# Hash attention and PReLU MLP: signs of a pair in one ScalarE pass placed by transfers, weights rounded with integer adds, GpSimd's adding transfer and small copies moved to VectorE

## The chip, the cores and the metric

The kernel runs on one core of a Trainium2 chip. The core has a matrix engine (TensorE, with its weight loads shown apart as PEld), VectorE (DVE), ScalarE (ACT), GpSimd (POOL) and SyncE (SP), which here only issues transfers. The metric is the device time of one execution in microseconds, the median of several runs. A profile of one execution gives, for every instruction, its engine, source line, start and duration, and for every transfer its time from issue to landing.

## The reference

Attention in which a query sees only the keys whose six hash bits equal its own, followed by a two-layer MLP with a per-channel PReLU:

```python
batch, n_heads, seq, head_dim = (4, 8, 768, 64)          # proj: (64, 6)
q_bits = (np.einsum('bhsd,dk->bhsk', q, proj) > 0)
k_bits = (np.einsum('bhsd,dk->bhsk', k, proj) > 0)
mask = q_bucket[:, :, :, None] == k_bucket[:, :, None, :]   # bucket: the six bits as a number
scores = np.where(mask, scale * q @ k.T, -1000000000.0)
attn = softmax(scores);  attn_out = attn @ v
x = attn_out.transpose(0, 2, 1, 3).reshape(B * S, H * D)    # 3072 x 512
h = x @ w_in                                                # 512 x 2048
g = np.maximum(h, 0.0) + alpha * np.minimum(h, 0.0)
out = (g @ w_out).astype(np.float32)                        # 2048 x 512
```

The two weight matrices come as 64-bit floats; everything else is fp32. The kernel therefore rounds the weights to fp32 itself, from the low and high 32-bit words of each number.

## The kernel before

All that runs is `fast_path`; a flag that it computes would start `general_path` for inputs out of range, which these inputs are not.

**Attention.** The work goes over 16 pairs of heads (4 batches x 4 pairs), numbered from 0 here. Two heads share the 128 partitions. For each pair, in the order in which each engine runs it:

- `turn` (L669) transposes `q` and `k` on TensorE into `qT` and `kT`, two pairs ahead.
- `hash_bits` (L689), one pair ahead, multiplies them with the projection into one two-bank PSUM tile `hs`, in blocks of 32 rows that hold `k` and `q` of the two heads, the blocks of the second half of the sequence swapped between heads. Then signs are taken: `qb` and `kb` are +-1 numbers in bf16. ScalarE does it for all pairs from 1 on in seven instructions, four for `qb` (L712) and three for `kb` (L723), since each block must land at its own partitions. Pair 0 (`engine is DVE`) uses ScalarE for `qb` and VectorE for `kb` (L719).
- `scores` (L726) makes 12 cells of 128 keys x 384 queries. In each cell a bf16 product of the signs and the fp32 product of `qT` and `kT` (L734) are added in PSUM, then ScalarE takes the exponential (L737). Cells go key block by key block, and for each both query halves: cell 0 needs the first half of `qb`, cell 1 the second half; cells 6 to 11 need the second half of `kb`. Score tiles, transposes, hash products and row sums share three two-bank PSUM tiles in rotation.
- The row sums of the exponentials are added up on VectorE: `add_first` (L743), `add_third` (L754), `add_last` (L749), `add_total` (L758). In `add_first` from pair 1 on, GpSimd also issues a transfer that adds half of the third block into `accp` (L747), so `add_third` covers only the other half.
- `attend` (L762) multiplies with `v` (L770); `totals` (L776) sums `accd` over keys on TensorE (`sm`, L784); `divide` (L789) turns the sums into factors with VectorE transposes, reciprocals, four 32x12 copies on GpSimd (L806, L807) and a multiplication (L817), and stores `x`.

**Weights.** Between these steps, two of 32 pieces of 128x512 weights are rounded per pair. A piece goes through `load_weight` (L561), `weight_abs` (L574, on ScalarE except for the first two), `weight_clamp` (L583), `weight_parts` (L589) and `weight_sum` (L600). `weight_parts` shifts the absolute value of the high word into fp32 form (L594), takes its exponent (L597) and scales the low word with it (L598); `weight_sum` adds the two in fp32 (L619) and puts the sign in (L624). `weight_group` (L630) stores finished groups of `w_out` (L636) and queues sums and stores of groups of `w_in`.

**MLP.** After the last pair the two products are computed with a seven-product scheme in blocks, from the stored `x`, `w_in` and `w_out`. The change doesn't touch this stage.

**Order.** Compute instructions keep the written order on each engine (`do` is `keep_in_program_order`). Transfers are placed by the scheduler; SyncE issues them strictly in its own order, and each waits on SyncE for its data and buffers, so that one waiting transfer holds all behind it. Tiles come from pools with a fixed number of buffers (two unless stated); a tile's buffer is taken over only when the users of its last tile are done.

Of the kernel before, what the change touches and what calls it, by code (L numbers as in the profile page):

```python
# [8 lines left out]
F32 = mybir.dt.float32  # L9
BF16 = mybir.dt.bfloat16  # L10
U32 = mybir.dt.uint32
AF = mybir.ActivationFunctionType
ALU = mybir.AluOpType

# [392 lines left out]
def fast_path(  # L407
# [12 lines left out]
    nc = tc.nc  # L420
# [80 lines left out]

    def setup():

        zero = pool.tile([P, 512], BF16, name="zero", bufs=1)
        do(DVE.memset(zero, 0.0))
        do(DVE.memset(wh, 0.0))
        for s in range(2):
            nc.sync.dma_start(wh[D * s : D * s + D, :NB], proj)
        nc.sync.dma_start(alpha16, moe_alpha.rearrange("(t p) -> t p", p=P))
        make_identity(nc, ident)  # L510
        do(DVE.memset(ones, 1.0))

        ps = psum_av.tile([P, 2, 512], F32, name="nil", tag="av")
        nil.append(lambda: do(PE.matmul(ps[:, 0], zero[:, :P], zero, start=True, stop=True)))
        for i in range(7):
            nil[0]()

        do(DVE.memset(hb, 0.0))
        for r in range(0, P, 32):
            do(DVE.memset(hb[r : r + 2 * NB], 1.0 if r % D else -1.0))  # L520
            do(DVE.memset(hb[r : r + NB], -1e-37))

        do(DVE.tensor_scalar(hb_k[:, 0:1], hb, -1.0, None, op0=ALU.mult))
        do(DVE.memset(hb_k[:, 1:2], 0.0))
        for r in range(0, P, 32):
            do(DVE.memset(hb_k[r : r + 2 * NB, 1:2], 0.5))
        for t in pts:
            do(POOL.memset(t[:, :, :, CW : CW + 1], 1.0))
        for t in qbs:
            do(POOL.memset(t, 0.0))  # L530
# [36 lines left out]
    def halves(i):  # L567
        words = raw[i].bitcast(U32).rearrange("p (f t) -> p f t", t=2)
        return words[:, :, 0], words[:, :, 1]
# [4 lines left out]
    def weight_abs(i, engine=None):  # L574
        i = order[i]
        lo, hi = halves(i)
        wx[i] = pool.tile([P, 512], F32, name=f"wx{i}", tag="wx")
        if engine is DVE:
            do(DVE.tensor_scalar(wx[i].bitcast(U32), hi, 0x7FFFFFFF, None, op0=ALU.bitwise_and))
            return  # L580
        do(ACT.activation(wx[i], hi.bitcast(F32), AF.Abs))

# [5 lines left out]

    def weight_parts(i):  # L589
        i = order[i]  # L590
        lo, hi = halves(i)
        x = wx[i]
        wr[i] = r = pool.tile([P, 512], F32, name=f"wr{i}", tag="wr", bufs=1)
        do(DVE.tensor_scalar(  # L594
            x.bitcast(U32), x.bitcast(U32), 3, 0xC0000000, op0=ALU.logical_shift_left, op1=ALU.bitwise_xor,
        ))
        do(DVE.tensor_scalar(r.bitcast(U32), x.bitcast(U32), 0x7F800000, None, op0=ALU.bitwise_and))  # L597
        do(DVE.scalar_tensor_tensor(r, lo, 2.0 ** -52, r, op0=ALU.mult, op1=ALU.mult))  # L598

    def weight_sum(i):  # L600


        i = order[i]
        lo, hi = halves(i)
        x, r = wx[i], wr[i]
        if i < HW:
            n, m = divmod(i, 4)
            if m == 0:
                wst[n] = pool.tile([P, NM, 4, P], F32, name=f"wsi{n}", tag="wsi")
            slot = (0, 5, 1, 2)[m]  # L610
            dst = wst[n][:, slot].rearrange("p i f -> p (i f)")
        else:
            n, m = divmod(i - HW, 2)
            if m == 0:
                wst[HW + n] = pool.tile([P, 4, DM // 2], F32, name=f"wso{n}", tag="wso")
            w = wst[HW + n]
            dst = w[:, 0:4:3] if m == 0 else w[:, 1:3]
        turned = i < HW and m == 3
        do(DVE.scalar_tensor_tensor(  # L619
            r, x, -1.0 if turned else 1.0, r, op0=ALU.mult, op1=ALU.subtract if turned else ALU.add,  # L620
        ))
        if i >= HW:
            hi, r = (t.rearrange("p (a f) -> p a f", a=2) for t in (hi, r))
        do(DVE.scalar_tensor_tensor(  # L624
            dst.bitcast(U32), hi, 0x80000000, r.bitcast(U32), op0=ALU.bitwise_and, op1=ALU.bitwise_xor,
        ))

    sums_due = []

# [59 lines left out]
    def hash_bits(pi, halves=BOTH, engine=None):  # L689

        if halves.start == 0:
            bits["q", pi] = qbs[pi % 2]
            bits["k", pi] = pool.tile([P, S], BF16, name=f"kb{pi}", tag="kb")
        ps = {"k": two_banks(f"hs{pi}")}
        ps["q"] = psum_av.tile([P, 2, 512], F32, name=f"hsq{pi}", tag="av") if engine is DVE else ps["k"]
        for half in range(halves.start, halves.stop):
            for name in "qk" if engine is DVE else "kq":
                for s in range(2):  # L700
                    r, c = D * s, D * (s ^ half) + 32 * "kq".index(name)

                    for t, c in [("k", c)] + ([("q", c ^ D)] if engine is DVE and name == "q" else []):
                        do(PE.matmul(  # L704
                            ps[t][c : c + 32, half if t == "k" or engine is not DVE else 0, :CW], wh[r : r + D],
                            tr[name, pi][r : r + D, half * CW : (half + 1) * CW], start=True, stop=True,
                        ))
        for half in range(halves.start, halves.stop):
            cols = slice(half * CW, (half + 1) * CW)
            for s in range(2):  # L710
                c = D * (s ^ half ^ (engine is DVE)) + 32
                do(ACT.activation(  # L712
                    bits["q", pi][D * s : D * s + 32, cols], ps["q"][c : c + 32, 0 if engine is DVE else half, :CW], AF.Sign, bias=hb[c : c + 32],
                ))

            for to, c, n in [(0, 0, P)] if half == 0 else [(0, D, D), (D, 0, D)]:
                dst, src = bits["k", pi][to : to + n, cols], ps["k"][c : c + n, half, :CW]
                if engine is DVE:
                    do(DVE.tensor_scalar(  # L719
                        dst, src, hb_k[c : c + n, 0:1], hb_k[c : c + n, 1:2], op0=ALU.is_gt, op1=ALU.subtract,  # L720
                    ))
                else:
                    do(ACT.activation(dst, src, AF.Sign, bias=hb[c : c + n]))  # L723


    def scores(pi, cells):  # L726
# [16 lines left out]
    def add_first(pi):  # L743
        accp[pi] = pool.tile([P, 2 * NCH, CW], F32, name=f"accp{pi}", tag="accp", bufs=1)
        do(DVE.tensor_tensor(accp[pi], p(0), p(1), op=ALU.add))  # L745
        if pi:
            nc.gpsimd.dma_start(accp[pi][:, 2:], p(2)[:, 2:], accum_op=ALU.add)  # L747

    def add_last(pi):  # L749
        accd[pi] = pool.tile([P, 2 * NCH, CW], F32, name=f"accd{pi}", tag="accd", bufs=1)  # L750
# [1 line left out]
        do(DVE.tensor_tensor(accd[pi], accd[pi], p(5), op=ALU.add))  # L752

    def add_third(pi):  # L754
        n = 2 if pi else 4
        do(DVE.tensor_tensor(accp[pi][:, :n], accp[pi][:, :n], p(2)[:, :n], op=ALU.add))

    def add_total(pi):  # L758
        do(DVE.tensor_tensor(accd[pi], accd[pi], accp[pi], op=ALU.add))  # L759
# [29 lines left out]
    def divide(pi, between=lambda: None):  # L789

        b, hp = pairs[pi]
        n = HW2 // 32
        a = pool.tile([P, NCH, HW2], F32, name=f"st{pi}", tag="st", bufs=1)
        r = pool.tile([P, NCH, n], F32, name=f"rc{pi}", tag="rc")
        rr = pool.tile([P, NCH, 2, n], F32, name=f"rr{pi}", tag="rr")
        d = pool.tile([P, NCH, CW], F32, name=f"dn{pi}", tag="dn", bufs=1)
        for g in range(NCH):
            do(DVE.transpose(a[:, g], sums[pi][:, g, :HW2]))  # L800
        do(DVE.tensor_scalar(r, a.rearrange("p g (n w) -> p g n w", w=32)[:, :, :, 0], S * EPS, None, op0=ALU.add))
        for h in range(2):
            do(DVE.reciprocal(rr[:, :, h], r))
        for q0 in (0, D):
            q1 = q0 + 32
            do(POOL.tensor_copy(rr[q0 : q0 + 32, :, 1], rr[q1 : q1 + 32, :, 1]))  # L806
            do(POOL.tensor_copy(rr[q1 : q1 + 32, :, 0], rr[q0 : q0 + 32, :, 0]))  # L807
        vsum[pi] = pool.tile([P, 1], F32, name=f"vs{pi}", tag="vs")
        do(DVE.tensor_scalar(vsum[pi], av[pi][:, 0, CW : CW + 1], EPS, None, op0=ALU.mult))
        between()  # L810
        do(DVE.transpose(
            d.rearrange("p g w -> p (g w)"),
            rr.rearrange("p g h n -> p (g h n)").unsqueeze(2).to_broadcast([P, 2 * NCH * n, 32]),
        ))

        x = mid.tile([P, NCH, CW], F32, name=f"x{pi}", tag="x", bufs=1)
        do(DVE.scalar_tensor_tensor(x, av[pi][:, :, :CW], vsum[pi], d, op0=ALU.add, op1=ALU.mult))  # L817
        nc.sync.dma_start(x_s[b, hp], x.rearrange("p g w -> p (g w)"))
# [471 lines left out]
```

## Time and profile before

| | |
|---|---|
| median of 3 runs | 893.71 us (893.67 to 894.51) |
| profiled execution, span from first to last instruction | 892.6 us |
| busy in the span: TensorE, VectorE, ScalarE, GpSimd | 882.5, 756.4, 407.2, 46.2 us |
| attention stage, one pair | 20.6 us, 16 pairs up to 338 us |
| transfers: SyncE's queue, GpSimd's queue | 123.64 MB, 14.29 MB |
| granted TensorE clock | 0.998 of full speed |

In a line of groups or of a timeline, `out<-in` are tile names without numbers, followed by the shape; `xN` is a count. In a line of a timeline the first two numbers are the start and the duration in us, and brackets give idle time before the instruction and who ended it. A line of waits gives who waited for whom, the total in us, how many times and the longest. `SPq` is SyncE issuing a transfer; its duration is the issue alone. Durations of matmuls are modelled, and a busy TensorE is not one at its peak.

### The profile page before, as it was taken

Reading aid. Unit: us, or ns where it says so; the run is one execution under the profiler, and the core shown is the slowest. Engines: PE = TensorE matmul, PEld = TensorE weight load, DVE = VectorE, ACT = ScalarE, POOL = GpSimd, SP = SyncE. Lnnn points to the kernel's source line nnn. Section 1 sums busy time; section 2 is a strip of 40 time slices with the busy share of each in tenths; the row PEclk is TensorE's granted clock in tenths of the full one; section 3 lists DMA queues with packets and bytes.
Section 4 is the critical chain, followed back from the end, with each engine's and each line's share of the span. In section 5 each row is a group of like instructions: output and inputs, shape, how many; then the busy total and the mean of one; then the engine's idle time right before and its main releaser. Section 6 shows DMA issues by size and latency. Waiting matters only on the chain.

```text
span 892.6 us, 15369 instructions
## 1 busy us (share of the span) xinstructions
PE 882.5 (99%) x5886; PEld 594.4 (67%) x5886; DVE 756.4 (85%) x1266; ACT 407.2 (46%) x726; POOL 46.2 (5%) x109
## 2 busy tenths in 40 slices
PE   9999999999999999999999999999999999999996
PEld 5444445555554445557997557997557997556996
DVE  6888988989999987899898678988668988768986
ACT  7888888888888862222112222112222112222111
POOL 1000000100110001110000000000000000000000
PEclk9999999999999999999999999999999999999999
DMA  8565586686796826587334334333425242530242
GB/s 231 138 164 137 160 231 167 173 237 191 205 291 175 229 69 217 179 292 282 136 104 135 137 125 153 133 122 103 168 96 182 96 158 81 166 108 0 95 149 68
DMA packets 124978, 140.17 MB, mean 157 GB/s; under 512 B 77776, under 2 KB 109024, under 8 KB 121312
## 3 DMA queue, kind: packets, MB, share of 16 engines
q1 hardware_dynamic: 116096, 123.64, 44.2%
q0 software_dynamic: 6384, 14.29, 6.5%
q10 hardware_dynamic: 2416, 1.18, 0.5%
q8 instruction: 48, 0.79, 0.4%
q14 instruction: 34, 0.28, 0.1%
HBM read 104.87 MB, written 28.31 MB: 149 GB/s over the span
## 4 chain that ended last, share of the span: by engine, by line
PE 93%; DVE 5%; issue 1%; DMA 1%; ACT 0%; SPq 0%; ACTq 0%; DVEq 0%
PE sc L734 17%; PE av L770 13%; PE f_0a L870 2%; PE z_4a L870 2%; PE z_7a L870 2%; PE z_3a L870 2%; PE z_6a L870 2%; PE z_5a L870 2%; PE f_4a L870 2%; PE f_3a L870 2%; PE f_2a L870 2%; PE f_1a L870 2%; PE z_2a L870 2%; PE f_5a L870 2%; PE z_1a L870 2%; PE f_7a L870 2%
## 5 line engine op out<-in xcount | busy, mean ns | idle before, releaser
L737 ACT ACTIVATE pt<-sc 128x768 f32<-128x768 f32 x192 | 154.9, 812 | 37.9 <-PE sc L734 37.4
L734 PE MATMUL sc<-qT,kT 64*128 64x384 f32 x768 | 155.1, 482 | 0.0
L770 PE MATMUL av<-pt,vn 128*32 128x385 f32 (+1 forms) x1536 | 127.4, 486 | 0.0
L770 PEld LDWEIGHTS av<-pt,vn 128*32 128x32 f32 x1536 | 48.7, 109 | 71.1 <-issue 70.1
L734 PEld LDWEIGHTS sc<-qT,kT 64*128 64x128 f32 x768 | 68.0, 187 | 39.2 <-issue 39.2
L923 DVE TENSOR_TENSOR g<-g,g 128x384 f32<-128x384 f32 x128 | 68.4, 555 | 2.2
L734 PE MATMUL sc<-qb,kb 64*128 64x384 bf16 x384 | 62.9, 323 | 0.2 <-DVE kb L719 0.2
L987 DVE TENSOR_TENSOR gs<-g,gs 128x768 f32<-128x768 f32 x56 | 53.3, 952 | 1.0
L987 DVE TENSOR_TENSOR gs<-g 128x768 f32<-128x768 f32 x56 | 53.3, 952 | 0.0
L979 DVE TENSOR_TENSOR ws<-wl 128x512 f32<-128x512 f32 x56 | 38.5, 687 | 17.1 <-DMA wl<-w_out_s 16.0
L919 DVE SCALAR_TENSOR_TENSOR g<-h,alpha 128x384 f32<-128x384 f32 x32 | 19.7, 616 | 24.8 <-ACT h L912 24.8
L734 PEld LDWEIGHTS <-kb 64*128 64x128 bf16 x384 | 18.9, 94 | 27.8 <-issue 4.4
L745 DVE TENSOR_TENSOR accp<-pt,pt 128x1536 f32<-128x1536 f32 x16 | 28.1, 1758 | 10.5 <-ACT pt L737 10.5
L712 ACT ACTIVATE qb<-hs,hb 32x384 bf16<-32x384 f32 x60 | 34.4, 573 | 1.1 <-PE hs L704 0.2
L752 DVE TENSOR_TENSOR accd<-accd,pt 128x1536 f32<-128x1536 f32 x16 | 28.1, 1759 | 1.7
L751 DVE TENSOR_TENSOR accd<-pt,pt 128x1536 f32<-128x1536 f32 x16 | 28.0, 1752 | 0.0
L759 DVE TENSOR_TENSOR accd<-accd,accp 128x1536 f32<-128x1536 f32 x16 | 28.0, 1751 | 0.0
L723 ACT ACTIVATE kb<-hs,hb 64x384 bf16<-64x384 f32 (+1 forms) x45 | 26.0, 577 | 0.6
L870 PE MATMUL f_0a<-x,wi 128*128 128x384 f32 x64 | 23.5, 489 | 0.0
L870 PE MATMUL f_4a<-x,wi 128*128 128x384 f32 x64 | 23.3, 486 | 0.0
L870 PE MATMUL f_5a<-x,wi 128*128 128x384 f32 x64 | 23.3, 486 | 0.0
L870 PE MATMUL f_6a<-x,wi 128*128 128x384 f32 x64 | 23.3, 486 | 0.0
(351 smaller groups left out, 1775.1 us busy)
## 6 DMA issues: line engine op xcount, KB each, us to landing
wi<-w_in_s SPq DMA_DIRECT2D x32, 896.0 KB, 4.7
wl<-w_out_s SPq DMA_DIRECT2D x16, 1024.0 KB, 4.8
wl<-w_out_r SPq DMA_DIRECT2D x12, 1024.0 KB, 4.8
raw<-in_moe_w_out_dram SPq DMA_DIRECT2D x16, 512.0 KB, 5.0
raw<-in_moe_w_in_dram SPq DMA_DIRECT2D x16, 512.0 KB, 4.5
w_in_s<-wsi SPq DMA_DIRECT2D x16, 448.0 KB, 5.6
vn<-in_v_dram SPq DMA_DIRECT2D x16, 384.0 KB, 4.8
x_s<-x SPq DMA_DIRECT2D x16, 384.0 KB, 4.4
```

The source lines that it names most:

```text
L712: do(ACT.activation(bits["q", pi][D * s : D * s + 32, cols], ps["q"][c : c + 32, 0 if engine is DVE else half, :CW], AF.Sign, bias=hb[c : ...
L734: do(PE.matmul(sc[:, s, :CW], what["k", pi][r, ks], what["q", pi][r, qs], start=first, stop=not first,))
L737: do(ACT.activation(pts[kc][:, g, :, :CW], sc[:, :, :CW], AF.Exp, scale=SCALE / DOWN))
L745: do(DVE.tensor_tensor(accp[pi], p(0), p(1), op=ALU.add))
L751: do(DVE.tensor_tensor(accd[pi], p(3), p(4), op=ALU.add))
L752: do(DVE.tensor_tensor(accd[pi], accd[pi], p(5), op=ALU.add))
L759: do(DVE.tensor_tensor(accd[pi], accd[pi], accp[pi], op=ALU.add))
L770: do(PE.matmul(av[pi][D * s + t : D * s + t + 32, g, :w], nat["v", pi][:, s, kc * D + t : kc * D + t + 32], pts[kc][:, g, s, :w], start=(k ...
L870: do(PE.matmul(self.ps[bank], self.left(left, k), self.right(right, k), start=start and k == 0, stop=k == self.nk - 1, skip_group_check=no ...
L923: do(DVE.tensor_tensor(new_g(b, to)[:, i], g_m[b, x][:, i], g_m[b, y][:, i], op=ALU.subtract))
L979: do(DVE.tensor_tensor(t, w2[b, n, x], w2[b, n, y], op=op))
L987: do(DVE.tensor_tensor(t, g2[b, n, x], g2[b, n, y], op=ALU.subtract))
```

## The change

- **Signs.** From pair 1 on, one ScalarE instruction takes the signs of the whole 128x768 `hs` tile into a new tile `raw` (blocks 0 and 2 of a 128x1152 tile whose blocks 0 and 1 are `kb`). Block 0 is the first half of `kb` in place. Four transfers on SyncE's queue place the `q` rows in `qb`, two place the second half of `kb`. The tile has one buffer instead of two.
- **Weights.** `weight_abs` gets a second ScalarE instruction, which scales the low word to an integer of 0 to 8. `weight_parts` keeps only the shift; its exponent and scaling passes go. `weight_sum` merges the sign into the shifted high word and then adds the two as 32-bit integers. `wr` has two buffers instead of one.
- **Row sums.** The adding transfer of GpSimd goes; `add_third` covers the whole block on VectorE.
- **Factors.** The four small copies in `divide` run on VectorE.
- **Memory.** A tile of zeros of the start shares a buffer with `st`.

```diff
@@ setup, weight_abs, weight_parts, weight_sum
-        zero = pool.tile([P, 512], BF16, name="zero", bufs=1)
+        zero = pool.tile([P, 512], BF16, name="zero", tag="st", bufs=1)
...
+        wr[i] = pool.tile([P, 512], I32, name=f"wr{i}", tag="wr")
+        do(ACT.activation(wr[i], lo, AF.Copy, scale=2.0 ** -29))
...
     def weight_parts(i):
         i = order[i]
+        x = wx[i].bitcast(U32)
+        turned = i < HW and i % 4 == 3
+        do(DVE.tensor_scalar(
+            x, x, 3, 0x40000000 if turned else 0xC0000000, op0=ALU.logical_shift_left, op1=ALU.bitwise_xor,
+        ))
...
-        wr[i] = r = pool.tile([P, 512], F32, name=f"wr{i}", tag="wr", bufs=1)
-        do(DVE.tensor_scalar(
-            x.bitcast(U32), x.bitcast(U32), 3, 0xC0000000, op0=ALU.logical_shift_left, op1=ALU.bitwise_xor,
-        ))
-        do(DVE.tensor_scalar(r.bitcast(U32), x.bitcast(U32), 0x7F800000, None, op0=ALU.bitwise_and))
-        do(DVE.scalar_tensor_tensor(r, lo, 2.0 ** -52, r, op0=ALU.mult, op1=ALU.mult))
...
+        x, r = x.bitcast(I32), wr[i]
+        if i >= HW:
+            hi, x, r = (t.rearrange("p (a f) -> p a f", a=2) for t in (hi, x, r))
         do(DVE.scalar_tensor_tensor(
-            r, x, -1.0 if turned else 1.0, r, op0=ALU.mult, op1=ALU.subtract if turned else ALU.add,
+            x.bitcast(U32), hi, 0x80000000, x.bitcast(U32), op0=ALU.bitwise_and, op1=ALU.bitwise_xor,
         ))
-        if i >= HW:
-            hi, r = (t.rearrange("p (a f) -> p a f", a=2) for t in (hi, r))
-        do(DVE.scalar_tensor_tensor(
-            dst.bitcast(U32), hi, 0x80000000, r.bitcast(U32), op0=ALU.bitwise_and, op1=ALU.bitwise_xor,
-        ))
+        do(DVE.tensor_tensor(dst.bitcast(I32), x, r, op=ALU.add))
@@ hash_bits
-            bits["k", pi] = pool.tile([P, S], BF16, name=f"kb{pi}", tag="kb")
+            kb = pool.tile([P, 3 * CW], BF16, name=f"kb{pi}", tag="kb", bufs=1)
+            bits["k", pi] = kb[:, :S]
+            bits["raw", pi] = kb.rearrange("p (a w) -> p a w", w=CW)
...
+        if engine is None:
+            raw = bits["raw", pi]
+            do(ACT.activation(raw[:, 0:3:2], ps["k"][:, :, :CW], AF.Sign, bias=hb))
+            for half in range(2):
+                for s in range(2):
+                    c = D * (s ^ half)
+                    cols = slice(half * CW, (half + 1) * CW)
+                    nc.sync.dma_start(bits["q", pi][D * s : D * s + 32, cols], raw[c + 32 : c + 64, 2 * half])
+                    if half:
+                        nc.sync.dma_start(bits["k", pi][D * s : D * s + D, cols], raw[c : c + D, 2])
+            return
...
-                else:
-                    do(ACT.activation(dst, src, AF.Sign, bias=hb[c : c + n]))
@@ add_first, add_third, divide
-        if pi:
-            nc.gpsimd.dma_start(accp[pi][:, 2:], p(2)[:, 2:], accum_op=ALU.add)
...
-        n = 2 if pi else 4
-        do(DVE.tensor_tensor(accp[pi][:, :n], accp[pi][:, :n], p(2)[:, :n], op=ALU.add))
+        do(DVE.tensor_tensor(accp[pi], accp[pi], p(2), op=ALU.add))
...
-            do(POOL.tensor_copy(rr[q0 : q0 + 32, :, 1], rr[q1 : q1 + 32, :, 1]))
-            do(POOL.tensor_copy(rr[q1 : q1 + 32, :, 0], rr[q0 : q0 + 32, :, 0]))
+            do(DVE.tensor_copy(rr[q0 : q0 + 32, :, 1], rr[q1 : q1 + 32, :, 1]))
+            do(DVE.tensor_copy(rr[q1 : q1 + 32, :, 0], rr[q0 : q0 + 32, :, 0]))
```

More of the change, by code (lines that the diff above doesn't have):

```diff
@@ L11 @@
 U32 = mybir.dt.uint32
+I32 = mybir.dt.int32
 AF = mybir.ActivationFunctionType
@@ L590, in weight_parts @@
         i = order[i]
-        lo, hi = halves(i)
-        x = wx[i]
-        wr[i] = r = pool.tile([P, 512], F32, name=f"wr{i}", tag="wr", bufs=1)
+        x = wx[i].bitcast(U32)
+        turned = i < HW and i % 4 == 3
         do(DVE.tensor_scalar(
-            x.bitcast(U32), x.bitcast(U32), 3, 0xC0000000, op0=ALU.logical_shift_left, op1=ALU.bitwise_xor,
+            x, x, 3, 0x40000000 if turned else 0xC0000000, op0=ALU.logical_shift_left, op1=ALU.bitwise_xor,
         ))
-        do(DVE.tensor_scalar(r.bitcast(U32), x.bitcast(U32), 0x7F800000, None, op0=ALU.bitwise_and))
-        do(DVE.scalar_tensor_tensor(r, lo, 2.0 ** -52, r, op0=ALU.mult, op1=ALU.mult))
     def weight_sum(i):
@@ L604, in weight_sum @@
         lo, hi = halves(i)
-        x, r = wx[i], wr[i]
+        x = wx[i]
         if i < HW:
@@ L617, in weight_sum @@
             dst = w[:, 0:4:3] if m == 0 else w[:, 1:3]
-        turned = i < HW and m == 3
+        x, r = x.bitcast(I32), wr[i]
+        if i >= HW:
+            hi, x, r = (t.rearrange("p (a f) -> p a f", a=2) for t in (hi, x, r))
         do(DVE.scalar_tensor_tensor(
-            r, x, -1.0 if turned else 1.0, r, op0=ALU.mult, op1=ALU.subtract if turned else ALU.add,
+            x.bitcast(U32), hi, 0x80000000, x.bitcast(U32), op0=ALU.bitwise_and, op1=ALU.bitwise_xor,
         ))
-        if i >= HW:
-            hi, r = (t.rearrange("p (a f) -> p a f", a=2) for t in (hi, r))
-        do(DVE.scalar_tensor_tensor(
-            dst.bitcast(U32), hi, 0x80000000, r.bitcast(U32), op0=ALU.bitwise_and, op1=ALU.bitwise_xor,
-        ))
+        do(DVE.tensor_tensor(dst.bitcast(I32), x, r, op=ALU.add))
     sums_due = []
@@ L717, in hash_bits @@
                 dst, src = bits["k", pi][to : to + n, cols], ps["k"][c : c + n, half, :CW]
-                if engine is DVE:
-                    do(DVE.tensor_scalar(
-                        dst, src, hb_k[c : c + n, 0:1], hb_k[c : c + n, 1:2], op0=ALU.is_gt, op1=ALU.subtract,
-                    ))
-                else:
-                    do(ACT.activation(dst, src, AF.Sign, bias=hb[c : c + n]))
+                do(DVE.tensor_scalar(
+                    dst, src, hb_k[c : c + n, 0:1], hb_k[c : c + n, 1:2], op0=ALU.is_gt, op1=ALU.subtract,
+                ))
     def scores(pi, cells):
```

## The prediction

> **What bounds the kernel now.** I read the page first, then the waits of TensorE, the windows of single pairs, and the timelines of TensorE, VectorE and SyncE inside one pair. From the page, busy time by engine:
>
> ```profile
> PE 882.5 (99%) x5886; PEld 594.4 (67%) x5886; DVE 756.4 (85%) x1266; ACT 407.2 (46%) x726; POOL 46.2 (5%) x109
> ```
>
> TensorE is busy 882.5 of 892.6 us. Busy can hide lost time, so the second view is the list of waits, TensorE's own:
>
> ```profile
> PE nil L514 <- DVE hb L518: 1.2, 1, 1.2
> PE sm L784 <- DVE accd L759: 0.6, 1, 0.6
> PE z_2c L870 <- DVE m L1008: 0.5, 1, 0.5
> PE tp_q L676 <- DMA qn<-in_q_dram: 0.3, 1, 0.3
> PE sc L734 <- DVE kb L719: 0.2, 1, 0.2
> ```
>
> In the whole run its matmuls wait 2.8 us for anything (total, times, longest). The rest of its idle time is the end of the run (its last matmul starts at 884.8). Third, two pairs of the attention stage by window (busy of PE, PEld, DVE, ACT, POOL):
>
> ```profile
> 134.88:155.49 20.61, 20.61 (x214) 10.39 (x216) 18.96 (x29) 18.04 (x27) 2.06 (x5) 1.00 0.60 156
> 279.12:299.70 20.58, 20.58 (x215) 10.36 (x216) 19.71 (x31) 18.07 (x27) 2.06 (x5) 1.00 0.64 174
> ```
>
> Every pair takes 20.6 us, all of it TensorE. VectorE (19.0 to 19.7) and ScalarE (18.0), which the change relieves, already fit inside. So relief is worth only what TensorE waits for them: of the five waits one is in reach, the 0.6 us before the row sums `sm` of pair 14. In the timeline of TensorE (pairs count from 0; I count times in a pair from its first score matmul):
>
> ```profile
> 310.26 7.96 PE L770 MATMUL av<-pt,vn 128*32 128x385 f32 x96
> 318.84 0.86 PE L784 MATMUL sm<-accd,ones 128*32 128x192 f32 x16 [0.62 <-DVE accd L759]
> 319.63 0.34 PE L734 MATMUL sc<-qb,kb 64*128 64x384 bf16 x2
> ```
>
> **What the Trainium skill says.** "VectorE: DVE Perf Modes", Specifications: VectorE computes in fp32, integers are exact only below 2^24. So the new integer add needs another form, and the built program does list it as a special instruction over 128x1024, twice the elements; no row of this trace has it. Mode 2×_1P there: two adjacent 16-bit elements can pass per cycle. That gives both ends of its cost below. "DMA: Bandwidth & Descriptors", Anatomy of one DMA: a semaphore wait stands on the issuing sequencer, not in the DMA engine. Same page, Queues, rings and completion order: each engine takes a queue's descriptors in ring order, and a completion lands after the earlier writes of that engine. The trace agrees: a weight load issued into an empty SyncE queue lands in 3.7 to 4.4 us (six of them), one just behind a weight store takes 5.0:
>
> ```profile
> raw<-in_moe_w_in_dram SPq DMA_DIRECT2D x1, 512.0 KB, 5.0
> ```
>
> **The change part by part.**
>
> TensorE: the same instructions in the same order; only its waits differ.
>
> ScalarE, per pair: out go four `qb` signs (0.573) and three `kb` signs (0.580, 2 x 0.575), 4.0 us; in come one 128x768 sign, 0.81 as the `qT` copy of that shape, and two copies of low words, 0.70 as the `wx` pass on the same strided words. Net -1.8 us of 18.0. Worth nothing: it idles 2.4 us before its exponentials anyway. The second copy must wait for `wr` (the integer add at +17.0); behind it stand one `wx` pass and the next exponentials at +21.7, so 4.7 us cover 1.4. In pair 0 the first copy stands ahead of nine exponentials and needs a load issued at 7.8 that lands 5.5 later, 13.3; ScalarE comes there at 13.7. Free; later by 1 us it would cost about 0.5, as three score banks give 0.5 of slack.
>
> VectorE, per pair: L597 and L598 go, 2 x (0.427 + 0.693) = -2.24. The sign merge costs what L624 cost, 0.69. The integer add stands in for L619 (0.688): at best 0.69 (512 cycles, as any 128x512 two-input row), at worst 1.22 (1024 at the slope between the 768 row, 0.952, and the 1536 row, 1.758). I take 0.69. `add_third` over all 1536 instead of 768: 1.758 - 0.953 = +0.81. Four 32x12 copies at about 0.1 (between the 0.06 memsets and the 0.2 reciprocals): +0.4, ahead of the 0.76 us that `add_first` waits for exponentials at +4.35, so hidden. Net -1.0.
>
> What TensorE can feel is the end of `add_total`, due before `sm` at +19.83. Before it ends at +19.03 (153.85 - 134.82). After: L597 and L598 of the second piece fall in that stretch (-1.19 by start to start), the wider third add is in it (+0.80), the integer adds about +0.05: +18.7. Slack 1.1 instead of 0.8. In pair 14, which has no transposes ahead of `sm`, the 0.62 wait falls to about 0.3: **-0.3 us**.
>
> GpSimd: 15 accumulating transfers and 64 copies go; nothing waited on them but 1.0 us of VectorE in the last pair, where TensorE ran on. Worth 0.
>
> SyncE: six new transfers per pair (15 pairs). This is the only place where a new wait reaches TensorE. Its order in the built program is: three `q` signs, the second weight load (waits for VectorE to be done with `raw`), in pairs 3, 6, 11, 13 also the store of `wso` (waits for the integer add), then `k`, `q`, `k`. The queue as it stands, pair 6:
>
> ```profile
> 144.22 0.33 SPq L565 DMA_DIRECT2D raw<-in_moe_w_out_dram  x1
> 152.21 0.38 SPq L636 DMA_DIRECT2D w_out_r<-wso  x1
> 152.68 0.46 SPq L565 DMA_DIRECT2D raw<-in_moe_w_in_dram  x1
> 153.23 1.52 SPq L498 DMA_DIRECT2D qn<-in_q_dram  x2
> ```
>
> SyncE sits still for 7.7 us, then 1 MB goes out at once, and the signs will be behind it. The three first signs go at +11.7 and are needed at +20.6: safe. Of the last three, the `q` one is needed by the second cell's second matmul, +20.6 + 0.82 = +21.4; the `k` ones not before the seventh cell, +25.4. In the ten other pairs with a load: it goes at +16.4 (end of the merge plus 0.1), lands 3.7 to 4.4 later, the sign 0.1 to 0.2 behind it, since its 24 KB are 0.1 us of data: +20.2 to +21.0. In time by 0.4 to 1.2 us. In the four store pairs the two come 0.7 us apart; back to back they now take from the first issue to the second landing 4.87, 5.47, 5.57 and 4.97 us (pairs 3, 6, 11, 13), mean 5.2. So 16.4 + 5.2 + 0.15 = +21.75, and with some 0.15 to start again, about 0.5 us late (0 to 1.4). A late sign stops all TensorE work behind it, and none is made up. 4 x 0.5 = **+2.0 us**. In pair 14 the store (2.8 to 3.3 alone) goes at +17.1: +20.5, where it is needed at +20.5; 0.1.
>
> Sum: -0.3 + 2.0 + 0.1 = +1.8, against the profiled 892.6 span: 894.4. The median is 893.71, 1.1 above the span, so **895.5**. The smallest change that a measurement of this kernel tells from none is about 0.2%, 1.8 us: the forecast stands on that edge.
>
> **The rivals.**
>
> *In time everywhere (not slower).* If the two weight transfers overlap more than now, since no 256-byte loads follow at once (those follow the signs), the landing is at +21.4 or before and only the -0.3 stays: 893.4, up to 894.5 for 0.2 late. For it: 4.87 and 4.97 are almost early enough. Against: all four would have to be. It decides at 5.0 us from first issue to second landing.
>
> *The integer add runs at one half-word a cycle.* +0.53 each; two stand before `add_total`, which then ends at +19.8: 14 x 0.1 at `sm`, +0.75 in pair 14; the store pairs' signs 1.06 later (4 x 1.5 = 6), the others 0.53 later (some 1 us in all). About +9: 902.8. For it: the doubled element count. Against: all operands are adjacent.
>
> *The plain pairs are late too.* If signs land 0.8 later than reckoned, because descriptors on the slowest engine queue up, ten pairs lose about 0.4 and four 1.2: +9, 898 to 903. For it: loads that follow other traffic took up to 6.8 us. Against: nothing stands before the load in the SyncE queue.
>
> *Faster.* Removing all of the 0.6 wait gives 893.1; beyond 0.2% nothing in the trace allows it.
>
> **How the numbers follow.** Late in the store pairs only: 0.46 (894.6 to 897.5; below the 0.2% edge 0.14, beyond 0.32). In time everywhere: 0.32. Slow add 0.08, plain pairs late 0.10, faster by something unseen 0.04. Slower 0.32 + 0.18 = 0.50, same 0.14 + 0.32 = 0.46, faster 0.04. The range runs from 893.1 (all of the small gain, half a microsecond below the median) to 900.5, leaving out most of the slow add and half of the plain-late case. The likeliest case alone spans 894.6 to 897.5.
>
> **What would show it.** TensorE's waits should list the scores waiting for transfers of `qb`, some 4 times, 0.1 to 1.4 each, in windows of 21.1 instead of 20.6 for pairs 3, 6, 11 and 13 only; `sm` after `accd` about 0.3. The integer add should read 0.69; at 1.2 the second rival holds. VectorE near 18.0 and ScalarE near 16.2 per pair. No waits on `qb` at all would make the first rival right, waits in every pair the third. A wait of exponentials for weight copies in pair 0 would be a thing I missed.

## The result, and the profile after

The changed kernel takes 897.56 us (median of five runs, 896.79 to 899.26) where the kernel before, timed beside it, takes 894.51 (893.67 to 895.59): a ratio of 1.0036, 95% interval 1.0024 to 1.0049. It is 3 us slower. The forecast was 895.5, "slower" at even odds, so side and cause were forecast and the size fell short. The profiled execution spans 895.8 us, 3.2 more than before.

The first view is the page's list of busy times by engine:

```profile
PE 884.2 (99%) x5886; PEld 598.5 (67%) x5886; DVE 746.8 (83%) x1266; ACT 379.5 (42%) x668; POOL 14.4 (2%) x30
```

VectorE has lost 9.6 us of work, ScalarE 27.7, GpSimd 31.8, and the kernel is longer. Busy shares alone would have told the opposite story. TensorE's waits (total, times, longest) tell the right one:

```profile
PE sc L742 <- DMA qb<-kb: 2.1, 4, 1.1
PE nil L515 <- DVE hb L519: 1.2, 1, 1.2
PE z_2c L875 <- DVE m L1013: 0.5, 1, 0.5
PE sm L789 <- DVE accd L764: 0.2, 1, 0.2
PE sc L742 <- DVE kb L729: 0.2, 1, 0.2
```

The first line is new: four times the scores wait for a transfer of `q` signs. The fourth line is what the change bought: the row sums `sm` of pair 14 wait 0.2 us instead of 0.6. In the timeline of TensorE at the first of the four places, the start of pair 4:

```profile
94.81 0.32 PE L742 MATMUL sc<-qb,kb 64*128 64x384 bf16 x1
95.56 0.32 PE L742 MATMUL sc<-qb,kb 64*128 64x384 bf16 x1 [0.43 <-DMA qb<-kb]
```

The second cell's first sign matmul runs, its second one, which reads the other half of `qb`, starts 0.75 later. The other three are at 158.04 (0.34), 261.69 (0.30) and 304.27 (1.06), the starts of pairs 7, 12 and 14. At the end of pair 14 stands what was shown of before:

```profile
314.05 7.96 PE L775 MATMUL av<-pt,vn 128*32 128x385 f32 x96
322.23 0.86 PE L789 MATMUL sm<-accd,ones 128*32 128x192 f32 x16 [0.22 <-DVE accd L764]
323.02 0.34 PE L742 MATMUL sc<-qb,kb 64*128 64x384 bf16 x2
```

By window (busy of PE, PEld, DVE, ACT, POOL), pairs 4 and 6:

```profile
93.99:115.34 21.35, 20.92 (x216) 11.35 (x212) 18.41 (x29) 16.12 (x23) 0.00 (x0) 1.00 0.51 149
135.95:156.56 20.61, 20.61 (x217) 10.37 (x214) 18.42 (x29) 16.16 (x23) 0.00 (x0) 1.00 0.51 151
```

A pair with all its signs in time takes 20.61 us as before; pairs 4, 7 and 12 take 21.35, 21.26 and 21.22; pair 14 takes 20.95, where it took 19.97. From first score to first score the stalls are 0.74, 0.65, 0.61 and, since the row sums of pair 14 give 0.40 back, 0.98 + 0.40 = 1.38: **3.4 us**. The wait that the list prints is about 0.3 less than what the pair loses each time. Up to the first score of pair 15 the changed kernel is 3.39 later (323.02 against 319.63): 3.38 of stalls, -0.40 at `sm`, and 0.39 that it had lost before pair 1 (32.01 against 31.62). That last piece is not put down to the change: of the eleven kernels profiled below, one has late loads at the start; the other ten reach pair 1 between 30.81 and 31.92, whichever part of the change they hold. Of the 0.39, pair 0 begins 0.16 later, after first hash matmuls that took 0.85 us here and 0.51 before for the same shape; the other 0.23 is lost within pair 0, and why is not shown.

Where the sign comes from is in SyncE's own timeline, pair 3 (first score at 73.39):

```profile
89.67 0.33 SPq L566 DMA_DIRECT2D raw<-in_moe_w_out_dram  x1
90.39 0.38 SPq L634 DMA_DIRECT2D w_out_r<-wso  x1
90.87 0.51 SPq L717 DMA_DIRECT2D kb<-kb  x1
91.43 1.22 SPq L715 DMA_DIRECT2D qb<-kb  x1
92.70 0.59 SPq L717 DMA_DIRECT2D kb<-kb  x1
```

The last `q` sign is the fourth of these five transfers, behind a load, a store and a `k` sign. From the list of transfers of that stretch (KB, median us from issue to landing; the `k` signs are two, 4.5 and 3.0):

```profile
raw<-in_moe_w_out_dram SPq DMA_DIRECT2D x1, 512.0 KB, 4.0
w_out_r<-wso SPq DMA_DIRECT2D x1, 512.0 KB, 4.7
...
kb<-kb SPq DMA_DIRECT2D x2, 48.0 KB, 3.7
qb<-kb SPq DMA_DIRECT2D x1, 24.0 KB, 4.1
```

Counted from the first score of pair 3: the store goes at +17.00 and lands at +21.75; the first `k` sign lands at +21.95, the `q` sign, issued at +18.04, at +22.14. It was needed at +21.42. That is 0.72 late, and pair 4 is 0.74 longer. The three groups whose prices the forecast had estimated (us busy, mean ns of one, then idle time before them):

```profile
L580 ACT ACTIVATE wr<-raw 128x512 int32<-128x512 uint32 x32 | 22.8, 712 | 17.2 <-issue 16.0 <-DVE wso L624 1.1
L710 ACT ACTIVATE kb<-hs,hb 128x768 bf16<-128x768 f32 x15 | 13.5, 902 | 0.7
L624 DVE CUSTOM_DVE_ANT_0 wsi<-wx,wr 128x1024 uint16<-128x1024 uint16 x16 | 11.1, 692 | 0.7
```

### The profile page after: what moved, and what is told of

The parts are those of the page before. It is cut to its first block, busy times and chain, and to the rows that moved or that the text cites. A ratio compares the mean times of both kernels' runs of the same rounds, so it can differ in the third digit from the quotient of the medians.

```text
span 895.8 us, 15331 instructions
## 1 busy us (share of the span) xinstructions
PE 884.2 (99%) x5886; PEld 598.5 (67%) x5886; DVE 746.8 (83%) x1266; ACT 379.5 (42%) x668; POOL 14.4 (2%) x30
## 4 chain that ended last, share of the span: by engine, by line
PE 84%; DVE 9%; issue 3%; ACT 2%; DMA 2%; SPq 0%; DVEq 0%; ACTq 0%
PE sc L742 12%; PE av L775 10%; PE f_0a L875 2%; PE z_4a L875 2%; PE z_7a L875 2%; PE z_3a L875 2%; PE z_6a L875 2%; PE z_5a L875 2%; PE f_4a L875 2%; PE f_3a L875 2%; PE f_2a L875 2%; PE f_1a L875 2%; PE z_2a L875 2%; PE f_5a L875 2%; DMA qb<-kb 2%
## 5 line engine op out<-in xcount | busy, mean ns | idle before, releaser
L742 PEld LDWEIGHTS sc<-qT,kT 64*128 64x128 f32 x768 | 70.0, 187 | 40.9 <-issue 40.7
L742 PE MATMUL sc<-qb,kb 64*128 64x384 bf16 x384 | 66.5, 323 | 2.4 <-DMA qb<-kb 2.1
L742 PEld LDWEIGHTS <-kb 64*128 64x128 bf16 x384 | 20.9, 94 | 25.9 <-issue 4.3
L580 ACT ACTIVATE wr<-raw 128x512 int32<-128x512 uint32 x32 | 22.8, 712 | 17.2 <-issue 16.0
L761 DVE TENSOR_TENSOR accp<-accp,pt 128x1536 f32<-128x1536 f32 x16 | 28.0, 1753 | 0.0
L805 DVE STREAM_TRANSPOSE st<-sm 128x192 f32<-128x192 f32 x32 | 10.3, 361 | 16.9 <-PE sm L789 16.9
L875 PE MATMUL f_1a<-x,wi 128*128 128x384 f32 x64 | 23.3, 486 | 0.0
```

The source lines that it names most:

```text
L742: do(PE.matmul(sc[:, s, :CW], what["k", pi][r, ks], what["q", pi][r, qs], start=first, stop=not first,))
L761: do(DVE.tensor_tensor(accp[pi], accp[pi], p(2), op=ALU.add))
L875: do(PE.matmul(self.ps[bank], self.left(left, k), self.right(right, k), start=start and k == 0, stop=k == self.nk - 1, skip_group_check=no ...
```

## The experiments

Theory A: a sign is late because it stands in one queue behind the store, while 1 MB of weight traffic goes through; the rest of the change costs nothing. Theory B: the sign transfers cost it by themselves. A third reading is between them: the DMA engines are busy with 1 MB at that moment, whichever queue a sign comes from. All ratios are to the kernel before, with 95% intervals; times in a pair count from its first score matmul, and the sign in question, the fourth `q` sign, is needed at +21.42.

### The signs alone

```diff
  kernel before, with hash_bits() of the changed kernel:
+ do(ACT.activation(raw[:, 0:3:2], ps["k"][:, :, :CW], AF.Sign, bias=hb))
+ ... six nc.sync.dma_start(...)
```

> The kernel before with the new signs alone: one ScalarE pass and six transfers on SyncE; weight arithmetic, adds and copies as before. Here the old weight arithmetic reads the raw piece until its last pass, so all six sign transfers stand in SyncE's queue ahead of the second weight load and of the store. Theory A (a sign loses time only where it stands behind weight traffic): no wait of scores for qb, 20.6 us in every pair, the 0.6 us wait of pair 14 stays; 0.2 us or less from the kernel before. Theory B (the sign transfers themselves cost it, whatever stands before them): waits on qb as in the changed kernel, 3 us or more above the kernel before.

894.59 us, ratio 1.0002 (0.9996 to 1.0009). No wait on `qb`, every pair 20.6, pair 14 waits 0.62 for `accd` as before. SyncE's timeline in pair 3 of this kernel (first score at 72.57):

```profile
84.32 1.85 SPq L717 DMA_DIRECT2D qb<-kb  x3
86.27 0.55 SPq L719 DMA_DIRECT2D kb<-kb  x1
86.87 0.60 SPq L717 DMA_DIRECT2D qb<-kb  x1
87.51 0.60 SPq L719 DMA_DIRECT2D kb<-kb  x1
...
89.97 0.38 SPq L636 DMA_DIRECT2D w_out_r<-wso  x1
```

The same six transfers, all ahead of the store. The fourth `q` sign goes at +14.3 and has landed at +18.0. Theory B falls: the signs are free where nothing stands before them.

### Everything but the signs

```diff
  changed kernel, with hash_bits() of the kernel before (seven sign instructions)
```

> The changed kernel with the old seven sign instructions: integer weights, adds and copies on VectorE stay. Theory A and B alike: no transfer of signs, so no wait on qb; the row sums of pair 14 wait about 0.2 instead of 0.6 us; 0.3 to 0.4 us below the kernel before. A rival, that the weight part costs time by itself (the 0.39 us that the changed kernel lost before pair 1 among it), would show 0.4 us or more above that, and a late first score of pair 1.

893.88 us, ratio 0.9994 (0.9986 to 1.0002). No transfers of signs, no waits on `qb`, `sm` waits 0.23, pair 1 starts at 31.21. So each half of the change alone costs nothing and the two together cost 3 us. They meet in SyncE's queue: the integer weights read the raw piece for the last time one instruction earlier (L621 instead of L624), its buffer is free earlier (in a pair without a store the load goes at +16.3, where it went at +17.45 before), and in the order of the built program the next raw load, and the store with it, then come ahead of the last three signs. That the earlier buffer is what made the scheduler choose this order is inferred from these two kernels, not tested by itself.

### Another queue for the signs, and another for the store

```diff
- nc.sync.dma_start(bits["q", pi]..., raw[...])     # and the k signs
+ nc.gpsimd.dma_start(bits["q", pi]..., raw[...])
```

> The changed kernel with the six sign transfers issued by GpSimd, whose queue is empty, so none stands behind a raw load or a store. Theory A: the four waits on qb go (3.4 us), the time falls to 0.3 to 0.5 us below the kernel before. Theory B (sign transfers share the DMA engines with 1 MB of weight traffic, whichever queue they come from): some of the four waits remains, 1 to 3 us above.

What this text calls theory B is the third reading above. 893.86 us, ratio 0.9993 (0.9984 to 1.0001), no waits on `qb`. GpSimd need not stand behind the load, so the fourth sign already goes at +14.1 and lands at +17.8. That is right for theory A, but it takes the sign out of the way of the 1 MB in time as well as in the queue. The next kernel doesn't:

```diff
- nc.sync.dma_start(w_out_r[:, :, n]..., wst[HW + n])
+ nc.gpsimd.dma_start(w_out_r[:, :, n]..., wst[HW + n])
```

> The changed kernel with the 512 KB store of w_out_r issued by GpSimd; in SyncE's queue the last signs then stand behind the raw load alone, also in the pairs with a store. If the loss is the order in one queue (first load, then store, then sign): the three waits of 0.6 to 0.7 us go and only that of pair 14 may stay in part; 0 to 1 us above the kernel before. If it is the 1 MB that the DMA engines share: the waits stay, 2 to 3 us above.

893.70 us, ratio 0.9994 (0.9986 to 1.0002), no waits on `qb`, also none at the start of pair 14. Pair 3 (first score at 73.07), SyncE and then GpSimd:

```profile
89.36 0.33 SPq L566 DMA_DIRECT2D raw<-in_moe_w_out_dram  x1
89.79 0.50 SPq L717 DMA_DIRECT2D kb<-kb  x1
90.34 0.58 SPq L715 DMA_DIRECT2D qb<-kb  x1
```

```profile
90.37 0.75 POOL L634 DMA_DIRECT2D w_out_r<-wso  x1 [48.15 <-DVE wso L624]
```

Here load, sign and store are issued within 1 us, and the same 1 MB is under way. The sign lands 3.2 us after its issue, at +20.5; the store lands at +21.6, after it. The sign also goes 0.8 earlier than in the changed kernel, but with the same 3.2 us from +18.04 it would, by this estimate, still land at +21.2 and in time. Sharing the engines alone is thus not what made it late; its place behind the store in one queue is needed for that. The Trainium skill, "DMA: Bandwidth & Descriptors", section Queues, rings and completion order, says that each DMA engine takes turns between the queues it has work for, packet by packet; a sign in a queue other than the store's landing 1.1 us before a store issued at the same moment agrees with that.

### More stores

```diff
+ # second piece of pairs 1, 4, 9 and 12
+ nc.sync.dma_start(spare[2 * n + m // 2].rearrange("a p d -> p a d"), two.rearrange("p a c d -> p a (c d)"))
```

> The changed kernel with four more 512 KB stores in SyncE's queue, to a spare tensor that nothing reads, at the same place (between the second raw load and the last three signs) in pairs 1, 4, 9 and 12, which have no store of w_out_r there. Theory A (load, then store, then sign in one queue makes the sign late): four more waits of scores on qb, at the start of pairs 2, 5, 10 and 13, 0.6 to 1.0 us each, 2.4 to 4 us above the changed kernel. A rival (the four late pairs are late for something else of theirs): no new waits, the time of the changed kernel.

903.32 us, ratio 1.0102 (1.0086 to 1.0117). TensorE's waits:

```profile
PE sc L749 <- DMA qb<-kb: 7.0, 8, 1.5
```

Eight waits instead of four, and the new ones where the new stores are: pairs 2, 5, 10 and 13 are 1.64, 1.82, 1.15 and 1.25 longer. In sum 5.9, against the 5.8 that the medians differ (903.32 - 897.56; 6.2 when each is taken against the kernel before timed beside it). The place is as expected and the size above the 0.6 to 1.0 named. The signs of pairs 1 and 4 landed 5.2 after their issue, 1.4 behind the store, where that of pair 3 is 0.3 behind its store. What these two share with the long stall of pair 14 in the changed kernel is tested last.

### One place forward

```diff
- order of the sign transfers: q q q | k q k
+ order of the sign transfers: q q q | q k k      (| is where load and store come)
```

> The changed kernel with the fourth q sign sent ahead of the k signs: in SyncE's queue it still stands behind load and store, one transfer (0.55 us of issue) earlier. If its landing is set by the 1 MB ahead of it, it lands at most 0.15 us earlier (48 KB less ahead) and the waits stay at 0.5 to 0.6 us, about 0.5 us less in sum; if it is set by when SyncE issues it, each wait of 0.6 to 0.7 shrinks to 0.1 or 0.2 and pair 14's 1.4 to 0.8, some 2.2 us less in sum, 1 us above the kernel before.

896.21 us, ratio 1.0024 (1.0015 to 1.0033). Issued at +17.44 instead of +18.04, the sign of pair 3 lands 0.19 behind the store instead of 0.38, at +21.88, and pair 4 is 0.48 longer instead of 0.74; pair 7, where the store itself took 0.2 longer, 0.71 instead of 0.65; pair 14 0.78 instead of 1.38. So it is what lies ahead in the queue that sets the landing, not the moment of issue: going 0.6 us earlier brought the landing 0.26 forward. The 48 KB of a `k` sign ahead of it were worth 0.2, near the 0.15 named for this case and far from the 0.5 that the other case asked for. Against the kernels before timed beside them, this one is 2.1 us slower and the changed kernel 3.05; the difference of 0.9 lies between the two sums named (0.5 and 2.2), and most of it is pair 14, for a reason that comes last. The profiled execution was the longest of this kernel's twelve (900.64): in it the stretch from +11.7 of pair 11 was late, SyncE's issues too, and one sign landed 6.7 us after its issue; single packets of 4 KB took up to 2.3 us there, where their median is 0.16. Why is not known. Its pair 12 is left out of the comparison.

### The load in another queue, and the load afterwards

```diff
- nc.sync.dma_start(raw[i], piece(i))
+ nc.gpsimd.dma_start(raw[i], piece(i))
```

> The changed kernel with the raw weight loads issued by GpSimd: in the pairs with a store, the last q sign stands behind the store alone, and the same 512 KB of load go at about the same time by another queue. If load and store are both needed ahead in the same queue: no waits on qb, 0 to 0.5 us below the kernel before. If the store alone makes it late: the waits stay, 0.5 us or more each, 2 us or more above.

905.66 us, ratio 1.0129 (1.0114 to 1.0145). TensorE's waits:

```profile
PE sc L742 <- DMA qb<-kb: 4.7, 4, 1.3
PE tp_q L674 <- DMA qn<-in_q_dram: 3.5, 1, 3.5
```

The second line is a side effect at the start: the first raw loads no longer stand behind the first `q` tiles, and pair 1 begins at 38.55. The first line answers the question: with the store alone ahead of the sign in its queue and the load in another, the waits are there and longer (pairs 4, 7 and 12 lose 1.65, 1.41 and 1.52; pair 14 as much as in the changed kernel). In pair 3 the store, now taking turns with the load, needs 5.8 us, lands at +22.84, and the sign behind it at +23.04. Is the load needed, then?

```diff
- load_weight(i + 4)        # ahead of add_total
+ load_weight(i + 4)        # after hash_bits(pi + 1)
```

> The changed kernel with the second raw weight load emitted after the signs: in the pairs with a store, SyncE's queue holds store, q sign, k sign, load. The store stands ahead of the sign as before, but no load is under way beside it. If the sign is late because 1 MB must pass before it: the store alone lands in about 3 us (2.8 to 3.3 elsewhere), the sign at +20.4, a microsecond early; no waits on qb, 0 to 0.5 us below the kernel before. If a store ahead in the queue makes it late by itself: waits of 0.4 us or more stay in the same four pairs, 2 us or more above.

893.75 us, ratio 0.9992 (0.9984 to 1.0000), no waits on `qb`. The stores of this kernel (the 2.8 is the median of its eight; the four in pairs 3, 6, 11 and 13 all took 2.8):

```profile
w_out_r<-wso SPq DMA_DIRECT2D x8, 512.0 KB, 2.8
```

The store stands ahead of the sign at the same moment (+17.01) and lands at +19.8 instead of +21.7, the sign at +19.97. So it takes both: a store ahead in the sign's queue, and a load under way beside it that stretches the store from 2.8 to 4.7 us.

### The signs on ScalarE's queue

```diff
- nc.sync.dma_start(bits[...]..., raw[...])
+ nc.scalar.dma_start(bits[...]..., raw[...])
```

> The changed kernel with the six sign transfers issued by ScalarE, right after its sign pass. They cost ScalarE some 3.4 us of issue a pair, about twice what the change took from it. Theory A, with ScalarE's time worth nothing: no waits on qb, no other new wait of TensorE, 0.2 to 0.5 us below the kernel before. If ScalarE's time does matter: scores or transposes wait for ScalarE, and it is slower by 0.3 us a pair or more, 4 us in all.

894.11 us, ratio 0.9999 (0.9991 to 1.0008), no waits on `qb`, `sm` 0.17. The issues take ScalarE 3.6 us a pair (in pair 3: 1.80 for three, then 0.60, 0.61 and 0.60), twice what the change had taken from it, and no wait of TensorE answers to them. The gain named did not show in the timing; that ScalarE's time is worth nothing here did.

### All weight traffic after the signs

```diff
- nc.sync.dma_start(w_out_r[:, :, n]..., wst[HW + n])      # in weight_group
- load_weight(i + 4)                                        # ahead of add_total
+ late.append(lambda: nc.sync.dma_start(w_out_r[:, :, n]..., wst[HW + n]))
+ # after hash_bits(pi + 1): the late store, then load_weight(i + 4)
```

> The changed kernel with both the store and the second raw load emitted after all six signs, everything still on SyncE. No sign has weight traffic ahead of it: no waits on qb, row sums of pair 14 waiting 0.2; 0.2 to 0.5 us below the kernel before. If the loads, now about 1 us later, come late for ScalarE's copy of their words: a new wait of scores or exponentials, 0.5 us or more.

893.77 us, ratio 0.9992 (0.9986 to 0.9999). TensorE's waits:

```profile
...
PE z_2c L875 <- DVE m L1013: 0.5, 1, 0.5
PE sm L789 <- DVE accd L764: 0.2, 1, 0.2
PE sc L742 <- DVE kb L729: 0.2, 1, 0.2
```

The line of the signs is gone and the row sums keep their 0.2. This is the changed kernel with nothing but two lines emitted later, and the only version whose interval lies below the kernel before, by 0.7 us at the median and barely.

The fourth `q` sign of pair 3 in one table (issue and landing; what pair 4 then takes above 20.60):

| kernel | ahead of it in its queue | store | sign | pair 4 longer by |
|---|---|---|---|---|
| changed kernel | load, store, `k` sign | +17.00, +21.75 | +18.04, +22.14 | 0.74 |
| one place forward | load, store | +17.00, +21.69 | +17.44, +21.88 | 0.48 |
| load by GpSimd | store | +17.02, +22.84 | +17.45, +23.04 | 1.65 |
| load after | store (no load beside it) | +17.01, +19.8 | +17.45, +19.97 | 0 |
| store by GpSimd | load, `k` sign | +17.30, +21.6 | +17.27, +20.5 | 0 |
| weights after | nothing | +17.01, +20.3 | +14.29, +17.4 | 0 |

In the first three rows the stall is the landing less 21.42, within 0.03 us; in the others the sign is early.

### What stood in pair 13

The sign of pair 13 in the changed kernel landed 1.12 us behind its store, where those of pairs 3, 6 and 11 are 0.34 to 0.38 behind, and the store was no slower than theirs (+17.02 to +21.6). The queues of the stretch from 302 to 303 us (packets, MB, share of the 16 engines):

```profile
q1 hardware_dynamic: 405, 0.27, 81.9%
q8 instruction: 1, 0.02, 5.8%
```

One packet of 16 KB from a queue of instructions takes one of the 16 engines for 0.93 us (5.8% of 16 us), with the last signs under way. The execution has 48 of them, some 12 us apart in the attention stage. To move them without moving anything else:

```diff
- for i in range(7): PE.matmul(ps[:, 0], zero[:, :P], zero)                 # 7 x 512 columns
+ for i in range(49): PE.matmul(ps[:, 0, :72], zero[:, :P], zero[:, :72])   # 49 x 72 columns
```

> The changed kernel with 49 matmuls of 72 columns in the place of the 7 of 512 with which TensorE warms up: 84 more instructions (each matmul has a weight load) and about the same time, everything else and every queue's order the same. A packet of the instruction queue comes about every 12 us, as often as TensorE takes in some 250 instructions, so these packets should come some 4 us earlier against the work. If such a packet is what made the sign of pair 13 1.1 us late behind its store: the one now at +3.5 us after that store's issue moves ahead of it, and pair 14 loses 0.6 to 0.7 us instead of 1.4; the one now at 264.3, after the sign of pair 11 has landed, moves to 3 to 4 us after that pair's store, and pair 12 loses 1.1 to 1.8 instead of 0.6. If it is something else of pair 13: the long stall stays at the start of pair 14.

897.76 us, ratio 1.0037 (1.0023 to 1.0051): the time of the changed kernel. The long stall changed places as expected. In the attention stage the packets come 1 to 6 us earlier against the work (4 in the median); none lies in the 8 us after the issue of pair 13's store, its sign lands 0.37 behind the store instead of 1.12, and pair 14 loses 0.85 (20.42 - 19.97 + 0.40) instead of 1.38. One now comes 3.6 us after pair 11's store was issued, in the stretch from 259.5 to 260.5:

```profile
q8 instruction: 1, 0.02, 5.5%
```

There the sign lands 0.78 behind instead of 0.38, the wait is 0.96 instead of 0.30, and pair 12 loses 1.27 (21.88 - 20.61) instead of 0.61. Pair 14 kept 0.2 more than expected, since its store too landed 0.2 later than in the changed kernel (4.9 us); pair 7 lost 0.93 instead of 0.65, also behind a store that landed 0.2 later, with no such packet near it.

Two earlier kernels agree. With the `q` sign one place forward and with the loads by GpSimd, the packet comes 4.4 and 4.8 us after pair 13's store, and what is held is the `k` sign behind the `q` sign, for which nothing waits yet: it lands 1.65 and 1.26 behind the store, where the same sign of pair 6 is 0.36 and 0.38 behind. That fits pair 14 losing 0.6 less with the `q` sign one place forward. In the kernel with more stores, the two signs that were 1.4 behind have such a packet 4.2 and 4.0 us after their store's issue, and one that was 0.90 behind has one at 3.9; another is 0.88 behind without one, so not every lag is explained.

## Why the prediction was right, step by step

- **What bounds it**: held. TensorE sets every pair; taking work from VectorE, ScalarE and GpSimd moved the time by the one wait in reach. That the relief of ScalarE is worth nothing is shown by the kernel with the signs on ScalarE, which gave it more work than it had lost; with everything but the signs, which keeps the relief of VectorE and GpSimd, no pair from 1 on but 14 is shorter than before. The case held likeliest (0.46) is the one that came, though "slower" was only an even chance.
- **The wait of pair 14**: forecast about 0.3, measured 0.22, worth -0.40 instead of -0.3. `add_total` of pair 6 ends at +18.65 (forecast +18.7).
- **The integer add**: forecast 0.69, measured 0.692. The rival of one half-word per cycle (1.22) falls. Sizes off that cost nothing: the sign pass 0.90 instead of 0.81, the small copies 0.165 instead of 0.1, VectorE relieved by 0.6 us a pair instead of 1.0. The copy of words was 0.71 (0.70).
- **SyncE's order and where it is late**: held, shown by undoing the order in four ways (store away, load later, both later, signs in another queue). The windows were named wrongly: the sign sent in pairs 3, 6, 11 and 13 is waited for at the start of the next pair, so the long windows are 4, 7, 12 and 14.
- **Plain pairs and pair 14's own signs in time**: held. With a load alone ahead, signs of pairs 1 to 12 landed 0.5 to 1.2 us before they were needed (forecast 0.4 to 1.2), pair 14's at 323.4, needed 0.5 later (forecast: just then). The rival with plain pairs late falls, and so does the one with all in time.
- **The size, 4 x 0.5 = 2.0**: this term failed; it measured 3.38. Two parts of it were small. First issue to second landing was 5.4 (16.28 to 21.7) instead of 5.2. And "the sign 0.15 behind, since its 24 KB are 0.1 us" left out the `k` sign between store and `q` sign, 48 KB: the sign was 0.34 to 0.38 behind, and 0.19 when sent ahead of the `k` sign. Two more went the other way: the load was issued at +16.3 instead of +16.4, and starting again took 0.03 instead of 0.15. That makes 0.6 to 0.7 a stall, 0.1 to 0.2 above the forecast, at three places; that it came so near is in part these errors offsetting each other. The fourth was 1.38, at the end of the range of 0 to 1.4: a packet of instructions stood there, of which the sum had no term, and it went to another pair when the packet did.
- **From the span to the median**: the forecast added 1.1 us, the median of three runs less the span of one execution that was not the median one. Every run on record takes 1.7 to 1.9 us more than its own span. With five runs the median before is 1.9 above the profiled span, and the changed kernel's 1.8 above its own. Of the 2.1 us that the forecast fell short, 1.4 are in the span, most of it the stalls (1.3), and 0.7 here.
- **Readings that were loose without effect**: loads behind other traffic took up to 8.1 us before (the one at 249.06), not 6.8; and of the four loads just behind a store, two took 5.0 and 5.1, the other two 4.4 and 4.5.

## What to carry to other kernels

Before putting a small transfer that something waits for on a queue, write down what stands ahead of it in the built order, in bytes, and at what time it is needed: here a 24 KB transfer behind a 512 KB store landed 0.2 to 0.4 us after it, and later still where an instruction packet came between. Two edits that are each free can cost time together, because one of them frees a buffer earlier and so moves a large transfer ahead of the other's small one; undoing them one at a time does not show the cause, reading the queue's order does. The repair that worked here is the place in the queue, by emitting the large transfers later or by taking another queue, not a faster engine.

## What the runs showed that was not expected

**Instruction packets.** TensorE's own instruction stream delays transfers (48 packets for its 11,772 matmuls and weight loads): where a 16 KB packet of some 0.9 us came between a store and the sign behind it, the sign landed 0.4 to 1.1 us later than without, and moving the packets by adding 84 TensorE instructions took 0.53 us from the stall of one pair and put 0.66 on another's.

**Issue of small transfers.** A sign costs its queue 0.5 to 0.6 us to issue, where a 512 KB load costs 0.33. Single ones take longer: 1.09 to 1.24 behind load and store, and up to 1.28 where no store stands ahead. With nothing ahead a sign lands in 1.8 us.

**Spans of single profiles.** From the first score of pair 15 to the end, the kernels here took between 572.7 and 574.9 us in their one profiled execution, though the code of that stage is the same in all; the kernel with everything but the signs, 574.9, is no slower than the others in its timed runs. The stalls are therefore summed only up to the first score of pair 15.
